# One scale per weight matrix, tiles split into their predecessor's slot, weight loads on SP, and a mixture product that goes through PSUM

## The chip, the core and the metric

The kernel runs on one core of a Trainium2 chip. The core has a matrix engine (PE, with its weight loads shown apart as PEld), three engines for elementwise work (DVE, ACT, POOL) and a queue for transfers (SP). ACT can issue transfers too. Each engine runs its own list of instructions in order, and semaphores make one wait for another. The metric is the device time of one execution in microseconds; lower is better. The kernel before takes 1015.41 us (median of 3 runs, 1015.3 to 1017.15).

## What is computed

Attention over 8 batches of 12 heads, 448 tokens and head size 64, and behind it a gated two-layer block with a token shift. Cut to what matters:

```python
def _attn_ref(q, k, v, g_q, g_k):
    q_n, k_n = (rmsnorm(q, g_q), rmsnorm(k, g_k))
    scores = scale * np.matmul(q_n, k_n.transpose(0, 1, 3, 2))
    attn = np.exp(scores - np.max(scores, axis=-1, keepdims=True))
    attn = attn / (np.sum(attn, axis=-1, keepdims=True) + 1e-09)
    return np.matmul(attn, v)

def _moe_ref(x, mu_k, mu_r, w_k, w_v, w_r):      # x: (8, 448, 768)
    x_prev = np.concatenate([np.zeros((B, 1, D)), x[:, :-1, :]], axis=1)
    xk = mu_k * x + (1.0 - mu_k) * x_prev
    xr = mu_r * x + (1.0 - mu_r) * x_prev
    k = np.maximum(xk @ w_k, 0.0)                # w_k: 768 x 1024
    v = k * k @ w_v                              # w_v: 1024 x 768
    r = 1.0 / (1.0 + np.exp(-(xr @ w_r)))        # w_r: 768 x 768
    return r * v
```

The three weight matrices arrive as float64, seen by the kernel as pairs of 32-bit integers. Products are made from two float16 parts of each operand (high and low), so every product of the block is three matmuls: high by high, high by low, low by high.

## The kernel before

The work is written as generators, one for each strand: loads of q and k, their norms (`stats`, `preps`), `scores`, `expo` and `probs`, `vpreps`, `attends`, the mixtures (`mixk`, `mixr`, `mix`), the weights (`wload`, `weights`, `wsplit`) and the block itself (`moe`). A planner (`Plan`) holds a clock for every engine and a price for every instruction. At each step it takes, of all strands, the instruction with the earliest key (engine free and operands ready, less a tenth of the strand's priority) and records it. So the order on each engine is fixed when the program is built, and any change of prices, strands or priorities moves instructions everywhere.

PE has to do, batch by batch: scores and products with v (attention), then for the block the products **K** (`xk` by w_k, 144 matmuls a batch), **R** (`xr` by w_r, 126) and **V** (`kk` by w_v, 168). `moe` (L1078) starts K of the first batch when its six mixtures and all eight tiles of w_k are there, and R of the first batch only when all 20 tiles of the three matrices are split (L1113, `wdone == NW`).

The weights come in 20 tiles of 128 columns: 8 of w_k, 6 of w_r, 6 of w_v. `wload` has ACT issue two transfers for each tile into buffers `raw` (two of its own; for w_k two more inside the tile `kk`, which is not needed yet). `weights` decodes each half: POOL takes the low bits out of a byte, ACT makes a float32 of the top word into a PSUM bank of the share `mm`, DVE joins both into a buffer `wf`. `wsplit` then finds one scale for each tile: PE forms the tile's product with itself, DVE takes its diagonal (`dg`), PE sums it by a matmul with ones, DVE takes the maximum and makes a power of two (`WSC`). Last, ACT and DVE (or, for the tiles in `POOL_TILES`, POOL, ACT and POOL) scale the tile and split it into its high and low parts, `wkh` and `wkl` and so on, which the block reads with a stride.

A mixture (`mix`, L951) is four instructions for each of 96 pieces of 128x448: POOL multiplies the shifted x by a column into `df`, DVE adds the other product onto it (both operands in SBUF), ACT makes the high part, POOL the low part.

The PSUM has eight banks. `Share` lets the strands hold some of them: five for scores (`sc`), two for the block and the decode (`mm`), two for products with v, norms of v and weights of w_k (`ot`).

Of the kernel before, what the change touches and what calls it, by code (L numbers as in the profile page):

```python
# [1 line left out]

# [29 lines left out]
WF_BUFS = 2  # L32
# [6 lines left out]
LOW_TILES = range(0, 20)  # L39
POOL_TILES = range(1, 14)  # L40
# [48 lines left out]
WB_A = 'ot'  # L89
WB_B = 'mm'  # L90
# [5 lines left out]
W_GAP = 10e3  # L96
# [108 lines left out]

class Plan:
    LAT = 35

    def __init__(self, tc):
        self.tc = tc  # L210
        self.clk = dict.fromkeys(("PE", "DVE", "ACT", "POOL", "SP"), 0.0)
        self.last, self.use, self.threads = {}, {}, []
        self.form, self.dma_free, self.acc, self.n = None, {"SP": 0.0, "ACT": 0.0}, False, 0
        self.held = {"DVE": [], "POOL": []}

# [13 lines left out]
    def spawn(self, gen, prio=0):  # L229
        th = [gen, prio, None, 0.0]  # L230
        self.threads.append(th)
        self.advance(th)
# [92 lines left out]
    def run(self):  # L325
        while self.threads:
            best, key = None, None
            for th in list(self.threads):
# [11 lines left out]
                k = max(self.clk[th[2][0].eng] + wait, th[3] + slack) - PS * (th[1]() if callable(th[1]) else th[1])  # L340
# [100 lines left out]
def attn_moe_kernel(tc, q, k, v, g_q, g_k, mu_k, mu_r, w_k, w_v, w_r, out):  # L441
# [15 lines left out]
    banks = {n: Share(psum, *c) for n, c in (("sc", SC_SHARE), ("mm", MM_SHARE), ("ot", OT_SHARE))}  # L457
# [18 lines left out]
    for nm, kt, n in (("wk", ND, D_FF), ("wr", ND, D_MODEL), ("wv", NF, D_MODEL)):  # L476
        WS[nm] = (wpool.tile([P, kt, n], F16, name=nm + "h"), wpool.tile([P, kt, n], F16, name=nm + "l"))
# [9 lines left out]

    def WB(ci):
        return WB_A if ci < NF else WB_B

# [9 lines left out]
    def late():  # L500
# [21 lines left out]
        "raw": Ring(stage, [P, NF // 2, 2 * P], I32, "raw", RAW_BUFS, plan),  # L522
# [4 lines left out]
    for name, plan_ in (("kk", KK_LENT), ("xk", XK_LENT)):  # L527
# [5 lines left out]
        for n in plan_:  # L533
# [10 lines left out]
            if len(r.shape) == 3:  # L544
# [27 lines left out]
    def mu_stats():  # L572
        yield from until(lambda: st["lu"] >= 1 and len(WFT))
# [377 lines left out]
    def mix(b, d, which, dst, df, cnt):  # L951
# [5 lines left out]
        yield G_.tensor_scalar(out=df, in0=xp, scalar1=sc[:, j + ND:j + ND + 1], scalar2=0.0, op0=ALU.mult, op1=ALU.add)  # L957
        yield V.scalar_tensor_tensor(out=df, in0=xc, scalar=sc[:, j:j + 1], in1=df, op0=ALU.mult, op1=ALU.add)
# [17 lines left out]
    def wload():  # L976
        for nm, w, kt, c, ci in WT:
            hk = kt // 2
            for i in range(0, kt, hk):
                yield from until(lambda: st["g"] >= W_G0 + W_G1 * ci and st["lu"] >= (LEAD_W if ci < W_L1 else LEAD_W + 1 if ci < W_L2 else LEAD_W + 2))  # L980
                raw = yield from R["raw"].get(ci < NF)
                yield A.dma_start(out=raw[:, 0:hk, :], in_=w[i * P:(i + hk) * P, c * P:(c + 1) * P].bitcast(I32).rearrange("(i p) n -> p i n", p=P))
                RAW[ci, i] = raw

    def weights():
        for nm, w, kt, c, ci in WT:
            f = yield from R["wf"].get(ci < NF)
            fi = f.bitcast(I32)
            hk = kt // 2
            for i in range(0, kt, hk):  # L990
                yield from until(lambda: (ci, i) in RAW and st["tq"] >= GATE_W)
                raw = RAW.pop((ci, i))
                r4 = raw[:, 0:hk, :].rearrange("p i (n two) -> p i n two", two=2)
                top, low = r4[:, :, :, 1], r4[:, :, :, 0]
                zb = yield from banks["mm"].get()
                z = zb[:, 0:hk * P].rearrange("p (i n) -> p i n", n=P)
                zi = z.bitcast(I32)
                if ci in LOW_TILES:
                    yield G_.tensor_scalar(out=low, in0=raw.bitcast(mybir.dt.uint8)[:, 0:hk, :].rearrange("p i (n b) -> p i n b", b=8)[:, :, :, 3], scalar1=-15.5, scalar2=2.0 ** -5, op0=ALU.add, op1=ALU.mult)
                    yield A.activation(out=z, in_=top.bitcast(F32), func=AF.Prelu, scale=F64_EXP, alpha=F64_NEG)  # L1000
                    yield V.scalar_tensor_tensor(out=fi[:, i:i + hk, :], in0=zi, scalar=3, in1=low, op0=ALU.logical_shift_left, op1=ALU.bitwise_or)
                else:
                    yield A.activation(out=z, in_=top.bitcast(F32), func=AF.Prelu, scale=F64_EXP, alpha=F64_NEG)
                    yield V.tensor_scalar(out=zi, in0=zi, scalar1=3, scalar2=None, op0=ALU.logical_shift_left)
                    yield V.scalar_tensor_tensor(out=fi[:, i:i + hk, :], in0=low, scalar=29, in1=zi, op0=ALU.logical_shift_right, op1=ALU.bitwise_or)
                R["raw"].put(raw)
                banks["mm"].put(zb)
            WFT[ci] = f
            plan.spawn(wsplit(nm, kt, c, ci, f), wprio)
# [4 lines left out]
    def wsplit(nm, kt, c, ci, f):  # L1014
        cs = slice(c * P, (c + 1) * P)
        wh, wl = WS[nm]
        f = f[:, 0:kt, :]
        w16 = f.bitcast(BF16).rearrange("p i (n two) -> p i n two", two=2)[:, :, :, 1]
        pg = yield from banks[WB(ci)].get()
        yield [T.matmul(form=("w", 110 * kt), out=pg[:, 0:P], lhsT=w16[:, i, :], rhs=w16[:, i, :], start=(i == 0), stop=(i == kt - 1)) for i in range(kt)]  # L1020
        sc = WSC[:, ci:ci + 1]
        sci = sc.bitcast(I32)
        dg = small.tile([P, P], F32, name="dg", bufs=1)
        yield V.tensor_tensor(out=dg, in0=pg[:, 0:P], in1=ident, op=ALU.mult)
        yield T.matmul(form=("f", 400), out=pg[:, P:2 * P], lhsT=ones.broadcast_to([P, P]), rhs=dg, start=True, stop=True)
        yield V.tensor_reduce(out=sc, in_=pg[:, P:2 * P], axis=AX.X, op=ALU.max)
        banks[WB(ci)].put(pg)
        yield V.tensor_scalar(out=sci, in0=sci, scalar1=24, scalar2=23, op0=ALU.logical_shift_right, op1=ALU.logical_shift_left)
        yield V.tensor_scalar(out=sci, in0=sci, scalar1=-1.0, scalar2=float(204 << 23), op0=ALU.mult, op1=ALU.add)
        if ci in POOL_TILES:  # L1030
            yield G_.tensor_scalar(out=f, in0=f, scalar1=sc, scalar2=0.0, op0=ALU.mult, op1=ALU.add)
            yield A.copy(out=wh[:, :, cs], in_=f)
            yield G_.tensor_tensor(out=wl[:, :, cs], in0=f, in1=wh[:, :, cs], op=ALU.subtract)
        else:
            yield A.activation(out=wh[:, :, cs], in_=f, func=AF.Copy, scale=sc)
            yield V.scalar_tensor_tensor(out=wl[:, :, cs], in0=f, scalar=sc, in1=wh[:, :, cs], op0=ALU.mult, op1=ALU.subtract)
        R["wf"].put(WFT.pop(ci))
# [40 lines left out]
    def moe():  # L1078
        wk, wr, wv = WS["wk"], WS["wr"], WS["wv"]
        kk = xr = None  # L1080
        for b in range(B):
# [23 lines left out]
            for f in range(NF):  # L1105
                fs = slice(f * P, (f + 1) * P)
                z = yield from banks["mm"].get()
                yield from prod(z[:, 0:S], lambda i, a: wk[a][:, i, fs], lambda i, c: xk[:, i, c, :], ND, S)
# [10 lines left out]
            for blk in range(1 - b % 2, NT, 2):  # L1119
# [5 lines left out]
                for h in range(2):  # L1125
                    hs = slice(h * NH, (h + 1) * NH)
                    zr = yield from banks["mm"].get()
                    yield from prod(zr[:, 0:NH], lambda i, a: xr[:, i, a, ts], lambda i, c: wr[c][:, i, hs], ND, NH)
# [4 lines left out]
                    yield from prod(zv[:, 0:NH], lambda i, a: kk[:, i, a, ts], lambda i, c: wv[c][:, i, hs], NF, NH)  # L1133
# [41 lines left out]
def layouts(inputs):  # L1175
# [29 lines left out]
    return {"q": qd, "k": kd, "v": vd.reshape(b * h // 2, P, 2 * n * HD)}  # L1205
# [32 lines left out]
```

## Time and profile before

| what | value |
|---|---|
| median of 3 runs | 1015.41 us |
| profiled execution, its own time | 1015.21 us |
| span of its instructions | 1013.4 us |
| DVE, ACT, POOL busy | 812.7, 746.0, 691.8 us |
| matmuls recorded | 6082 |

The page of the profile gives, for each engine, the busy time in the span, and then the span cut into 40 slices of 25.3 us with one digit each (9 is 90 per cent or more busy). Other views group instructions by kind, list them in order of time, or give every engine's busy time in a stretch. The times of single instructions overlap at their ends on one engine, so a sum of durations is larger than the busy time: over this run DVE's durations sum to 962 us and it was busy for 812.7.

### The profile page before, as it was taken

The numbers are of one execution on the slowest core, as the hardware profiler recorded it, in microseconds if no ns is written. First come the engines' busy times: TensorE is split into PE (matmuls) and PEld (weight loads), VectorE is DVE, ScalarE is ACT, GpSimd is POOL, SyncE is SP. The second block draws the span as 40 slices with busy tenths as digits, with TensorE's granted clock in tenths as the row PEclk, the third lists the DMA queues.
The fourth block names the chain that finished last, engine by engine and source line by source line (L and its number), as shares of the span: only waits on it lengthen the run. The fifth ranks groups of instructions, "written<-read, shape, count | busy, mean of one in ns | idle before, by whom it ended". The sixth has DMA issues, their size and how long they took to land. (4 is left out here: it accounts for less than half of the span.)

```text
span 1013.4 us, 18593 instructions
## 1 busy us (share of the span) xinstructions
PE 926.0 (91%) x6082; PEld 485.8 (48%) x6082; DVE 812.7 (80%) x2260; ACT 746.0 (74%) x1756; POOL 691.8 (68%) x734
## 2 busy tenths in 40 slices
PE   2588869669999999999999999899999999999998
PEld 2354434335544555455545555355545454455564
DVE  5879998999998698979997998799997989763000
ACT  3667878878788789888887887878886988952311
POOL 2787889743798747877886859855987478556501
PEclk9878979869999999999999999999999999999999
DMA  7322349667788789569847977869858884640000
GB/s 248 119 80 86 118 120 221 170 166 169 172 165 168 143 197 203 133 152 201 207 105 173 214 158 161 161 131 201 175 126 177 186 183 110 146 107 32 1 32 32
DMA packets 371138, 148.17 MB, mean 146 GB/s; under 512 B 338272, under 2 KB 355168, under 8 KB 371040
## 3 DMA queue, kind: packets, MB, share of 16 engines
q1 hardware_dynamic: 351792, 129.20, 57.0%
q10 hardware_dynamic: 19248, 17.77, 5.9%
q8 instruction: 48, 0.79, 0.3%
q14 instruction: 50, 0.41, 0.1%
HBM read 51.98 MB, written 11.01 MB: 62 GB/s over the span
## 5 line engine op out<-in xcount | busy, mean ns | idle before, releaser
L273 PE MATMUL ps<-wvh,kk 128*128 128x384 f16 x896 | 233.1, 326 | 0.8 <-DVE nat L273 0.8
L273 ACT ACTIVATE ps<-ps,sums 128x448 f32<-128x448 f32 x294 | 181.9, 621 | 52.5 <-DVE sums L273 48.9
L273 PE MATMUL ps<-xk,wkh 128*128 128x448 f16 x768 | 210.5, 356 | 4.8 <-DVE wf L273 3.9
L273 DVE SCALAR_TENSOR_TENSOR nat<-ps,sums,nat 128x64 f16<-128x64 f32 x480 | 190.7, 439 | 19.2 <-ACT nat L273 17.8
L273 DVE TENSOR_REDUCE sums<-ps 128x1 f32<-128x448 f32 x336 | 193.7, 612 | 15.4 <-PE ps L273 15.1
L273 PE MATMUL ps<-wrh,xr 128*128 128x384 f16 x672 | 179.9, 331 | 2.1 <-DVE nat L273 2.0
L273 ACT ACTIVATE nat<-ps,sums 128x448 f16<-128x448 f32 (+1 forms) x272 | 167.8, 659 | 16.9 <-DVE sums L273 7.1
L273 PEld LDWEIGHTS <-kk 128*128 128x128 f16 (+1 forms) x1362 | 129.2, 98 | 98.7 <-issue 13.5
L273 PE MATMUL ps<-stk 64*128 64x448 f16 (+3 forms) x1104 | 134.2, 390 | 26.4 <-ACT xk L273 6.2
L273 PE MATMUL ps<-wvl,kk 128*128 128x384 f16 x448 | 146.0, 326 | 0.0
L273 PE MATMUL ps<-xk,wkl 128*128 128x448 f16 x384 | 136.5, 355 | 0.0
L273 PEld LDWEIGHTS <-xr 128*128 128x128 f16 x1008 | 96.4, 99 | 80.1 <-issue 16.9
L273 PE MATMUL ps<-wrl,xr 128*128 128x384 f16 x336 | 111.1, 331 | 0.0
L273 PEld LDWEIGHTS <-wkh 128*128 128x128 f16 x768 | 71.9, 99 | 81.6 <-issue 21.6
L273 POOL TENSOR_TENSOR o<-o,bsc 128x384 f32<-128x384 f32 x48 | 43.3, 902 | 88.3 <-DVE o L273 52.3
L273 DVE SCALAR_TENSOR_TENSOR o<-o,ps 128x384 f32<-128x384 f32 x56 | 30.5, 545 | 87.7 <-PE ps L273 59.2
L273 PE MATMUL ps<-pT,vh 128*64 128x448 f16 x588 | 93.8, 363 | 1.4 <-DMA pT<-nat 0.7
L273 ACT ACTIVATE o<-ps,bsc 128x128 f32<-128x128 f32 x144 | 45.6, 387 | 51.2 <-PE ps L273 33.1
L273 POOL TENSOR_TENSOR qk<-qk,ss 128x896 f32<-128x896 f32 x36 | 64.0, 1778 | 22.1 <-DVE ss L273 14.9
L273 PEld LDWEIGHTS <-stk 64*128 64x128 f16 x1008 | 35.0, 98 | 78.0 <-issue 35.5
L273 DVE SCALAR_TENSOR_TENSOR df<-x,bsc,df 128x448 f32<-128x448 f32 x68 | 61.0, 910 | 5.8 <-POOL df L273 5.7
L273 POOL TENSOR_TENSOR nat<-nat 128x448 f32<-128x448 f32 x41 | 48.2, 1175 | 23.6 <-ACT nat L273 17.1
(161 smaller groups left out, 1813.7 us busy)
## 6 DMA issues: line engine op xcount, KB each, us to landing
vf<-in_v_dram SPq DMA_DIRECT2D x48, 256.0 KB, 3.0
out_dram<-o SPq DMA_DIRECT2D x28, 384.0 KB, 2.7
qk<-in_k_dram SPq DMA_DIRECT2D x23, 448.0 KB, 4.4
qk<-in_q_dram SPq DMA_DIRECT2D x22, 448.0 KB, 4.3
raw<-in_moe_w_v_dram ACTq DMA_DIRECT2D x12, 512.0 KB, 4.2
raw<-in_moe_w_r_dram ACTq DMA_DIRECT2D x12, 384.0 KB, 3.3
kk<-in_moe_w_k_dram ACTq DMA_DIRECT2D x8, 384.0 KB, 3.9
raw<-in_moe_w_k_dram ACTq DMA_DIRECT2D x8, 384.0 KB, 3.7
```

What stands on the lines that cost most here:

```text
L273: r = op.fn(op.kw["out"], op.kw["value"]) if op.fn.__name__ == "memset" else op.fn(**op.kw)
```

## The change

1. **Scales.** The products of all tiles of a matrix with themselves are summed in one PSUM bank (w_k: four blocks of columns of one bank), and `wscale` makes one scale for the matrix when its last tile has been decoded. The three instructions on a diagonal and the matmul with ones run 3 times and not 20.
2. **Slots.** A decoded tile waits for its scale, so all tiles of a matrix must be held. Tile c is decoded, as float32, into the slot of the split tile c + 1, which has just its size; the last tile goes to a `wf` buffer (now one, not two). `wsplit` takes the tiles in order, so tile c is split into slot c when tile c - 1 has been read from there. The slots of a matrix are now one tile `wk` (`wr`, `wv`), laid out by tile, part, row block and column.
3. **Loads.** The host lays the weights out by tile, so that each half tile is one run in every partition, and SP issues these 40 transfers, not ACT.
4. **Decode.** POOL writes the low bits straight to the place of the result, not back into `raw`, and `raw` is free once POOL, ACT and DVE are through. The PSUM banks of the decode are a share of their own (`wz`, two), as are the sums (`pg`, one).
5. **Split.** The tiles that POOL splits are now every second one (10), before tiles 1 to 13 (13).
6. **Mixture.** The first product is made by ACT into a PSUM bank (share `df`, one); DVE reads it from there.
7. **Planner.** Up to 20 ns of seeded noise is added to each key, and `W_GAP` goes from 10e3 to 7e3, so that the weights' priority falls by less with each tile.

```diff
-WF_BUFS = 2
+WF_BUFS = 1
-LOW_TILES = range(0, 20)
-POOL_TILES = range(1, 14)
+WZ_SHARE = (2, 0)
+PG_SHARE = (1, 0)
+DF_SHARE = (1, 0)
+POOL_TILES = range(0, 20, 2)
-WB_A = 'ot'
-WB_B = 'mm'
-W_GAP = 10e3
+W_GAP = 7e3
...
+SEEDS = [641]
+AMP = 20.0
+SEG = 1e9
...
+        th[4] = self.noise()
...
-                k = max(self.clk[th[2][0].eng] + wait, th[3] + slack) - PS * (th[1]() if callable(th[1]) else th[1])
+                k = max(self.clk[th[2][0].eng] + wait, th[3] + slack) - PS * (th[1]() if callable(th[1]) else th[1]) + th[4]
...
-        WS[nm] = (wpool.tile([P, kt, n], F16, name=nm + "h"), wpool.tile([P, kt, n], F16, name=nm + "l"))
+        WS[nm] = wpool.tile([P, n // P, 2, kt, P], F16, name=nm)
...
-        yield G_.tensor_scalar(out=df, in0=xp, scalar1=sc[:, j + ND:j + ND + 1], scalar2=0.0, op0=ALU.mult, op1=ALU.add)
-        yield V.scalar_tensor_tensor(out=df, in0=xc, scalar=sc[:, j:j + 1], in1=df, op0=ALU.mult, op1=ALU.add)
+        pb = yield from banks["df"].get()
+        yield A.activation(out=pb[:, 0:S], in_=xp, func=AF.Copy, scale=sc[:, j + ND:j + ND + 1])
+        yield V.scalar_tensor_tensor(out=df, in0=xc, scalar=sc[:, j:j + 1], in1=pb[:, 0:S], op0=ALU.mult, op1=ALU.add)
+        banks["df"].put(pb)
...
-                yield A.dma_start(out=raw[:, 0:hk, :], in_=w[i * P:(i + hk) * P, c * P:(c + 1) * P].bitcast(I32).rearrange("(i p) n -> p i n", p=P))
+                yield SP.dma_start(out=raw[:, 0:2 * hk * P], in_=w[c, h].bitcast(I32))
...
+                f = WS[nm][:, c + 1].rearrange("p a i n -> p (a i n)").bitcast(F32)
...
+            yield [T.matmul(form=("w", 110 * kt), out=pg[:, c % nb * P:(c % nb + 1) * P], lhsT=w16[:, i, :], rhs=w16[:, i, :], start=(c == 0 and i == 0), stop=(last and i == kt - 1)) for i in range(kt)]
+            if last:
+                plan.spawn(wscale(nm, kt, ci - c, ci + 1, pg, nb * P), wprio)
...
+    def wscale(nm, kt, c0, c1, pg, w):
+        sc = WSC[:, c0:c0 + 1]
...
+        yield V.tensor_copy(out=WSC[:, c0 + 1:c1], in_=sc.broadcast_to([P, c1 - c0 - 1]))
+        for ci in range(c0, c1):
+            plan.spawn(wsplit(nm, kt, ci - c0, ci, ci + 1 == c1), wprio)
+
+    def wsplit(nm, kt, c, ci, last):
+        yield from until(lambda: st["wdone"] == ci)
+        sc = WSC[:, ci:ci + 1]
+        f = WFT[nm].rearrange("p i n -> p (i n)")[:, 0:kt * P] if last else WS[nm][:, c + 1].rearrange("p a i n -> p (a i n)").bitcast(F32)
+        hi, lo = (WS[nm][:, c, a].rearrange("p i n -> p (i n)") for a in range(2))
```

What this does to the order is seen best at three places. The first is PE's list around the first product K of the first batch. Before, it stands here, behind scores (`stk`) and the sum of one tile's diagonal (`dg`):

```order
L273 LDWEIGHTS stk_948
L273 MATMUL ps_1447<-stk_948 64x448
L273 MATMUL ps_1421<-dg,ones 128x128
L273 LDWEIGHTS wkh
L273 MATMUL ps_1509<-xk_104,wkh 128x448
```

Now it stands behind the product of the very last weight tile with itself (`wf_1500`, the sixth of w_v), three transposes and the third and last sum of a diagonal:

```order
L287 LDWEIGHTS wf_1500
L287 MATMUL ps_1190<-wf_1500 128x128
L287 MATMUL ps_1588<-ident,nat_1436 128x128 x3
L287 MATMUL ps_1190<-dg,ones 128x128
L287 LDWEIGHTS wk
L287 MATMUL ps_1627<-xk_101,wk 128x448
```

So all 20 tiles are decoded ahead of the first K, where before 12 were, and no more products or sums for weights stand between K and R. On PE's list, ahead of the first K stand 78 score matmuls before and now, and 48 products with v; ahead of the first R stand 162 score matmuls and 114 products with v before, and 114 and 70 now.

The second place is DVE's list at the end of the weights, which the first R waits for. Before, the last tile of w_v has its own diagonal, maximum and two steps of its scale in between attention's work:

```order
L273 TENSOR_TENSOR dg<-ps_2413,ident 128x128
L273 TENSOR_SCALAR bstat<-bstat 128x1
L273 SCALAR_TENSOR_TENSOR nat_2401<-ps_2355,sums_109,nat_2401 128x64
L273 SCALAR_TENSOR_TENSOR nat_2401<-ps_2355,sums_109,nat_2401 128x384
L273 TENSOR_REDUCE WSC<-ps_2413 128x1
L273 TENSOR_SCALAR sums_110<-ps_2404 128x2
L273 TENSOR_REDUCE sums_105<-ps_2436 128x1
L273 TENSOR_SCALAR WSC<-WSC 128x1
```

Now the last splits of w_v stand between the mixtures for R (`df` from `x` and a PSUM bank), with no scale left to make:

```order
L287 SCALAR_TENSOR_TENSOR wv<-wf_1500,WSC,wv 128x1024
L287 TENSOR_SCALAR WIN<-WSC 128x12
L287 TENSOR_SCALAR sums_106<-ps_1876 128x2
L287 SCALAR_TENSOR_TENSOR df_1919<-x_1227,bsc,ps_1920 128x448
L287 TENSOR_SCALAR WIN<-WIN,smu 128x6
L287 TENSOR_SCALAR WIN<-WIN,wsc 128x6
```

The row `WIN<-WSC` was number 535 of DVE's list and is now number 377. Up to and with the output scales of the first batch, the last DVE work ahead of the first R, DVE now has 400 instructions.

The third place is SP's list near the start. These rows are new between the loads of q, k and v: each weight load waits until its buffer has been decoded, and the loads below wait with it.

```order
L287 DMA qk_134<-in_q_dram 128x896
L287 DMA kk_100<-in_moe_w_k_dram 128x768 x2
L287 DMA raw_255<-in_moe_w_k_dram 128x768
L287 DMA raw_264<-in_moe_w_k_dram 128x768
L287 DMA qk_205<-in_k_dram 128x896
L287 DMA kk_100<-in_moe_w_k_dram 128x768
L287 DMA xk_101<-in_q_dram 128x896
```

Before, the weight loads stood in ACT's list, between its arithmetic, and SP's list held q, k and v one behind the other:

```order
L273 DMA vf_95<-in_v_dram 128x512
L273 DMA qk_119<-in_k_dram 128x896
L273 DMA qk_159<-in_q_dram 128x896
L273 DMA qk_180<-in_k_dram 128x896
L273 DMA xk_104<-in_q_dram 128x896
L273 DMA qk_315<-in_k_dram 128x896
```

What moved is the order in which SP comes to the q and k of the second and third group of heads: one to four weight transfers now stand ahead of each.

More of the change, by code (lines that the diff above doesn't have):

```diff
@@ L985, in weights @@
     def weights():
         for nm, w, kt, c, ci in WT:
-            f = yield from R["wf"].get(ci < NF)
-            fi = f.bitcast(I32)
[L989 to L1005, printed above, removed]
@@ new lines, in weights @@
+            if c == 0:
+                pg = yield from banks["pg"].get()
+            last = ci + 1 in (NF, NF + ND, NW)
+            nb = 4 if ci < NF else 1
+            if last:
+                wf = yield from R["wf"].get(ci < NF)
+                f = wf.rearrange("p i n -> p (i n)")[:, 0:kt * P]
+                WFT[nm] = wf
+            else:
+                f = WS[nm][:, c + 1].rearrange("p a i n -> p (a i n)").bitcast(F32)
+            fi = f.bitcast(I32)
+            for h in range(2):
+                yield from until(lambda: (ci, h) in RAW and st["tq"] >= GATE_W)
+                raw = RAW.pop((ci, h))
+                n = kt * P // 2
+                cols = slice(h * n, (h + 1) * n)
+                zb = yield from banks["wz"].get()
+                z = zb[:, 0:n]
+                yield G_.tensor_scalar(out=fi[:, cols], in0=raw.bitcast(mybir.dt.uint8)[:, 0:8 * n].rearrange("p (n b) -> p n b", b=8)[:, :, 3], scalar1=-15.5, scalar2=2.0 ** -5, op0=ALU.add, op1=ALU.mult)
+                yield A.activation(out=z, in_=raw[:, 0:2 * n].rearrange("p (n two) -> p n two", two=2)[:, :, 1].bitcast(F32), func=AF.Prelu, scale=F64_EXP, alpha=F64_NEG)
+                yield V.scalar_tensor_tensor(out=fi[:, cols], in0=z.bitcast(I32), scalar=3, in1=fi[:, cols], op0=ALU.logical_shift_left, op1=ALU.bitwise_or)
+                banks["wz"].put(zb)
@@ L1011, in inverse @@
     def inverse(o, i):
         return V.tensor_scalar(out=o.bitcast(I32), in0=i.bitcast(I32), scalar1=-1.0, scalar2=float(0x7F000000), op0=ALU.mult, op1=ALU.add)
[L1014 to L1021, printed above, removed]
-        sci = sc.bitcast(I32)
[L1023 to L1027, printed above, removed]
+    def wscale(nm, kt, c0, c1, pg, w):
+        sc = WSC[:, c0:c0 + 1]
+        sci = sc.bitcast(I32)
+        dg = small.tile([P, 4 * P], F32, name="dg", bufs=1)[:, 0:w]
+        yield V.tensor_tensor(out=dg.rearrange("p (b n) -> p b n", n=P), in0=pg[:, 0:w].rearrange("p (b n) -> p b n", n=P), in1=bcast(ident[:, :], w // P), op=ALU.mult)
+        yield T.matmul(form=("f", 200 + 1.7 * w), out=pg[:, 0:w], lhsT=ones.broadcast_to([P, P]), rhs=dg, start=True, stop=True)
+        yield V.tensor_reduce(out=sc, in_=pg[:, 0:w], axis=AX.X, op=ALU.max)
+        banks["pg"].put(pg)
@@ L1037, in wsplit @@
-        R["wf"].put(WFT.pop(ci))
+            yield A.copy(out=hi, in_=f)
+            yield G_.tensor_tensor(out=lo, in0=f, in1=hi, op=ALU.subtract)
+        else:
+            yield A.activation(out=hi, in_=f, func=AF.Copy, scale=sc)
+            yield V.scalar_tensor_tensor(out=lo, in0=f, scalar=sc, in1=hi, op0=ALU.mult, op1=ALU.subtract)
+        if last:
+            R["wf"].put(WFT.pop(nm))
         st["wdone"] += 1
```

52 lines of the change are left out of this document (29 added, 23 removed).

## The prediction

> **What bounds the kernel now.** I read the page first, for the engine that is nearly full and the part of the span in which it isn't.
>
> ```profile
> span 1013.4 us, 18593 instructions
> PE 926.0 (91%) x6082; PEld 485.8 (48%) x6082; DVE 812.7 (80%) x2260; ACT 746.0 (74%) x1756; POOL 691.8 (68%) x734
> PE   2588869669999999999999999899999999999998
> PEclk9878979869999999999999999999999999999999
> ```
>
> PE is busy for 91% of the span, and its digits fall below 9 almost only in the first ten slices, 250 us. There its granted clock is also below full. So I looked for what PE does there, in its list in order of time, at three places (start, length, and in brackets the idle time before it with what ended it):
>
> ```profile
> 141.01 0.91 PE L273 MATMUL ps<-xk,wkh 128*128 128x448 f16 x2 [3.90 <-DVE wf L273]
> 227.46 0.50 PE L273 MATMUL ps<-wrh,xr 128*128 128x384 f16 x1 [1.39 <-DVE nat L273]
> 1008.30 0.33 PE L273 MATMUL ps<-wvh,kk 128*128 128x384 f16 x1
> ```
>
> These are the first K, the first R and the last V. They cut the run into stages, and the view of busy time by stretch gives each engine's part in them (start:end, length, then busy us and instructions of each engine, granted clock, DMA share, GB/s).
>
> ```profile
> core 0: us, PE busy (x) PEld busy (x) DVE busy (x) ACT busy (x) POOL busy (x), PEclk, DMA share, GB/s
> 0.00:141.00 141.00, 93.55 (x531) 53.77 (x532) 117.70 (x337) 92.63 (x215) 99.38 (x132) 0.88 0.40 128
> 141.00:186.80 45.80, 41.90 (x253) 21.64 (x253) 39.11 (x101) 38.49 (x82) 43.12 (x42) 0.94 0.76 179
> 186.80:227.50 40.70, 24.56 (x152) 11.84 (x150) 37.55 (x109) 31.02 (x65) 22.57 (x25) 0.68 0.73 181
> 227.50:926.00 698.50, 683.34 (x4666) 351.32 (x4667) 609.90 (x1704) 565.70 (x1355) 496.28 (x506) 0.99 0.74 161
> 926.00:1008.60 82.60, 82.60 (x485) 47.24 (x483) 7.84 (x11) 18.14 (x43) 29.67 (x32) 1.00 0.05 20
> 1008.60:1013.40 4.80, 0.03 (x1) 0.00 (x0) 0.56 (x1) 0.00 (x0) 0.83 (x1) 1.00 0.20 82
> ```
>
> From the first R on, PE is the bound: 683.34 of 698.50 us, then all of 82.60, and a tail of 4.80 us. Ahead of it PE waits. The stretch from 186.8 us, where the last K of batch 0 has begun, to the first R is the worst: 40.70 us with 24.56 busy, at a clock of 0.68, while DVE is busy for 37.55. What PE waits for there is the weights, which DVE finishes in between attention. So the end is **the time of the first R, plus PE's work after it, plus the tail**. I work out each.
>
> **Term 1, the first K.** The order gives the first K the sixth mixture as its last operand, which is DVE instruction 335 now and was 338. The durations of what differs:
>
> ```profile
> L273 DVE SCALAR_TENSOR_TENSOR wf<-ps,raw 128x384 int32<-128x384 int32 x18 | 9.8, 547 | 0.1
> L273 DVE SCALAR_TENSOR_TENSOR wf<-ps,raw 128x512 int32<-128x512 int32 x12 | 8.2, 680 | 0.6 <-issue 0.4 <-POOL raw L273 0.2
> L273 DVE SCALAR_TENSOR_TENSOR wkl<-kk,WSC,wkh 128x768 f16<-128x768 f32 x1 | 1.0, 1008 | 0.0
> L273 DVE TENSOR_TENSOR dg<-ps,ident 128x128 f32<-128x128 f32 x20 | 5.6, 280 | 0.8 <-PE ps L273 0.8
> L273 DVE TENSOR_REDUCE WSC<-ps 128x1 f32<-128x128 f32 x20 | 5.7, 283 | 2.6 <-PE ps L273 2.5
> L273 DVE TENSOR_SCALAR WSC<-WSC 128x1 int32<-128x1 int32 x40 | 5.8, 144 | 0.2
> L273 DVE SCALAR_TENSOR_TENSOR df<-x,bsc,df 128x448 f32<-128x448 f32 x68 | 61.0, 910 | 5.8 <-POOL df L273 5.7
> L273 DVE SCALAR_TENSOR_TENSOR dfx<-x,bsc,dfx 128x448 f32<-128x448 f32 x28 | 31.6, 1130 | 4.1 <-POOL dfx L273 4.1
> L273 DVE SCALAR_TENSOR_TENSOR df<-x,bsc,df x68: 653/700/2564, 127.3 to 930.1; 128x448 f32<-128x448 f32 x68
> ```
>
> DVE gains 12 decodes of w_v halves (12 x 0.680) and 4 more of w_k and w_r (4 x 0.547), 10.3 us, and 6 splits of about 1.0 us. It loses 8 to 10 diagonals and maxima and 16 steps of scales (10 x 0.280 + 8 x 0.283 + 16 x 0.144, less 0.6 for a wide one: 6.8). The mixture's DVE part has a mean of 974 ns (68 x 910 and 28 x 1130) but a least of 653 and a median of 700 (last row): POOL's work lengthens it, since both of its operands are in SBUF. With one in PSUM no row here shows it; I bound it by 653 and the mean, 974, and take 660, near the least, because instructions that read PSUM show no such spread (547 and 680 above). Six mixtures: less 1.9 us. A few norms and copies more, about 4. Together about +12 us of durations; DVE's durations overlap (962 for 812.7 busy), so +10 us, and **the first K at 151 us**.
>
> The Trainium skill, SBUF — State Buffer, Who interferes with whom, says that a DVE instruction with two SBUF inputs contends with a GpSimd instruction that reads SBUF, and one with a single SBUF input doesn't. The trace agrees as far as it goes (653 to 2564 ns for two inputs); by that rule the 660 holds, without it the first R comes 4 us later (12 mixtures).
>
> **Term 2, from the first K to the first R.** Before, 45.80 us to the last K, then 40.70. In the new order nothing of weights is left for PE, and the R follows the last K directly. PE's groups in 141 to 186.8:
>
> ```profile
> L273 PE MATMUL ps<-wf 128*128 128x128 bf16 x28 | 2.4, 220 | 0.5 <-DVE wf L273 0.5
> L273 PE MATMUL ps<-dg,ones 128*128 128x128 f32 x8 | 1.7, 300 | 2.1 <-DVE dg L273 2.1
> L273 PE MATMUL ps<-ident,nat 128*128 128x128 f32 x14 | 2.2, 277 | 0.0
> ```
>
> Of the 45.80 us, 2.4 and 1.7 for weights with 2.6 of waits are gone, and a third of the transposes (0.8): 38 us. In these 38 us DVE has to do 65 instructions, with five splits of weights and six mixtures for R, where it did 101 in 45.8; it keeps up. ACT, 84% busy there, gets the mixtures' six products (3.5 us) and sheds tile splits. So I let PE set the pace: **the first R at 189 us**. Bounds: 176 if DVE alone counts (147 fewer instructions than the 547 to 227.5, 44 us less of 194.4 busy, at the same share of the time), and 201 if ACT's work to that point (about 143 us against 162.1) takes the same share of the time as now.
>
> **Term 3, from the first R to the last V.** Now 1008.6 - 227.5 = 781.1 us. Attention that stood ahead of the first R now stands behind it: 48 score matmuls, 44 products with v, 16 transposes. Their pace, from two places in PE's list:
>
> ```profile
> 237.05 0.38 PE L273 MATMUL ps<-pT,vh 128*64 128x448 f16 x2
> 239.26 0.34 PE L273 MATMUL ps<-wvh,kk 128*128 128x384 f16 x1
> 257.93 1.31 PE L273 MATMUL ps<-stk 64*128 64x448 f16 x12
> 259.17 0.34 PE L273 MATMUL ps<-wrh,xr 128*128 128x384 f16 x1
> ```
>
> 22 products in 2.21 us and 12 scores in 1.24, 0.1 us each: 9.2 us, and 16 transposes at a third of their 277 ns or so, 1.8. Term 3 is **792 us** if PE stays the bound. Whether it does is for ACT: 84 mixtures are left, each with an ACT product that no row shows. The nearest:
>
> ```profile
> L273 ACT ACTIVATE ps<-raw 128x384 f32<-128x384 f32 x20 | 10.6, 528 | 0.3 <-issue 0.3
> L273 ACT ACTIVATE ps<-raw 128x512 f32<-128x512 f32 x12 | 7.7, 638 | 1.3 <-DVE wf L273 0.9 <-DVE WSC L273 0.3
> 510.00:520.00 10.00, 10.00 (x65) 4.62 (x63) 9.84 (x24) 10.00 (x25) 10.00 (x9) 1.00 0.29 75
> ACT ps L273 <- DVE sums L273: 44.3, 40, 5.4
> ```
>
> They bound it by 528 and 638 ns; 580 for 448 columns. That is 49 us, and attention put off adds about 20 (16 exponentials and 16 copies of 0.62 to 0.66): ACT goes from 565.7 to 635 us of 710, from 81% to 89%. It can run that full: in 510 to 520 us ACT and PE are both busy for all of it, and its greatest wait (last row, 227 to 926 us) is for DVE's maxima, 44.3 us, on a DVE that is relieved (84 x 0.31 = 26 us). POOL loses 84 products of 0.66 us and more. I take nothing off or on for this; the rivals carry both ends.
>
> **The rest.** The last V to the end: 4.8 us. The planner's noise takes no time on the chip; its effect is in the order, which is counted. The 40 issues of weight loads leave ACT's list for SP's. One from ACT's queue in the order of time:
>
> ```profile
> 19.81 0.37 ACTq L273 DMA_DIRECT2D kk<-in_moe_w_k_dram  x1
> ```
>
> At 0.37 us they make 15 us of ACT's time ahead of 227 us; I take nothing for it, since PE and DVE set the pace there. **Sum: 189 + 792 + 4.8 = 986 us of span.** The profiled execution took 1015.21 for a span of 1013.4, so 1.8 more: **988 us**, against 1015.21 (and the median of 1015.41, the same within 0.2).
>
> **Rivals.**
>
> *Loads wait on SP* (15%). Weight loads now wait on SP for ACT's, POOL's and DVE's decode, and behind them stand q, k and v and later transposes. Against: their data are needed late, and SP mostly sits idle. For:
>
> ```profile
> qk<-in_k_dram SPq DMA_DIRECT2D x23, 448.0 KB, 4.4
> raw<-in_moe_w_k_dram ACTq DMA_DIRECT2D x8, 384.0 KB, 3.7
> ```
>
> A load takes 4.4 us and a weight half 3.7, so a load kept behind four of them comes some 15 us late; if that hits the first 150 us once, 1003 us. The Trainium skill, DMA: Bandwidth & Descriptors, Queues, rings and completion order, says that SP and ACT each have a ring on every DMA engine, consumed in ring order; so weights would now also hold up the data of the loads behind them. No run here shows that yet; by it this rival's price is the same 15 us.
>
> *ACT becomes the bound* (9%, slower). If ACT can't be busier than the 81% it has now, its 635 us take 784 and not 710, and the end is 988 + 74 = 1062. It decides at 86%: 635/0.86 = 738, 28 later, which eats the whole gain. The 10 of 10 us above speak against it.
>
> *The weights don't come earlier* (6%, slower). No tile is split before its matrix is whole, so if the last split of w_v is late the first R stays at 227 us, with 11 us of attention put off: 227.5 + 792 + 6.6 = 1026. Against it: DVE has 400 instructions up to there, and had 547.
>
> *Relief* (15%). PE's 15.2 us of idle time in 227.5 to 926 shrink by half with a DVE and POOL that block each other less, and the first R comes at 182: 974.
>
> *No effect* (5%): a gain of the start is lost later in new waits for PSUM banks, of which the decode, sums and mixtures hold four: within 2 us of 1015.
>
> **Numbers.** The forecast, 980 to 996, has 50%. The range leaves out the 20% of ACT, the late weights and no effect: 971 to 1012. A measurement of this kernel can tell about 0.2% from no change. Faster by more: 50 + 15 + 15 = 80%; the same 5%; slower 15%.
>
> **What would show it.** First K near 151 and first R near 189 us in PE's list; a clock above 0.9 and PE idle for no more than 5 us between them; DVE's mixture near 660 ns, ACT's near 580; ACT near 89% and PE still near 98% from the first R to the last attention; some 92 more attention matmuls there. A first R behind 201 us, or an ACT that ends PE's waits, would make it wrong.

## The result, and the profile after

The changed kernel takes **1022.59 us** (median of 4 runs, 1021.35 to 1023.0), the kernel before 1015.76 us in runs beside it (4 runs, 1015.3 to 1017.15): a ratio of 1.0063, 95% interval 1.0045 to 1.008. So it is slower by more than the 0.2% that can be told from no change, where 988 us and a gain had been forecast. The lines of the page that answer to those of before (the span, the busy time of each engine, and PE and its clock in 40 slices, now of 25.5 us):

```profile
span 1021.0 us, 18527 instructions
PE 918.5 (90%) x6048; PEld 482.0 (47%) x6048; DVE 785.4 (77%) x2200; ACT 792.6 (78%) x1850; POOL 605.5 (59%) x632
PE   2767868899899999898999999999999999999998
PEclk9798969999899999999999999999999999999999
```

PE has less to do than before (918.5 against 926.0 us), and DVE and POOL much less. The hole of the start ends a slice earlier. But behind the tenth slice PE's row, which had one 8 there (and the last slice), now has three. The first K and the first R of the changed kernel in PE's list, and its stages (start:end, length, busy us and instructions of each engine, granted clock, DMA share, GB/s):

```profile
157.93 0.55 PE L287 MATMUL ps<-xk,wk 128*128 128x448 f16 x1 [2.34 <-DVE df L287]
199.58 0.50 PE L287 MATMUL ps<-wr,xr 128*128 128x384 f16 x1
...
0.00:157.90 157.90, 100.26 (x580) 55.95 (x580) 130.44 (x336) 106.24 (x240) 102.45 (x137) 0.88 0.51 166
157.90:199.60 41.70, 37.45 (x212) 18.02 (x213) 36.23 (x76) 37.38 (x76) 36.78 (x32) 0.95 0.28 69
199.60:901.20 701.60, 665.68 (x4576) 341.32 (x4575) 605.89 (x1767) 619.79 (x1466) 430.17 (x425) 0.99 0.76 166
901.20:1016.20 115.00, 115.00 (x684) 66.74 (x683) 12.25 (x22) 29.20 (x71) 35.28 (x40) 1.00 0.05 21
1016.20:1021.00 4.80, 0.06 (x1) 0.00 (x0) 0.55 (x1) 0.00 (x0) 0.83 (x1) 1.00 0.20 82
```

And the stage from the first R to the last attention in the kernel before, cut in the same way (last attention at 906.8 us):

```profile
227.50:907.10 679.60, 664.44 (x4549) 339.93 (x4549) 603.98 (x1695) 560.24 (x1340) 488.72 (x495) 0.99 0.76 165
```

The first R comes at 199.6 us, 27.9 earlier. From there to the end of the last V the kernel before needs 781.1 us and this one 816.6, 35.5 more. Two parts make that up. PE's busy time there goes from 765.9 us (the prediction's rows) to 665.68 + 115.00 = 780.7: 14.8 more. And its idle time between the first R and the last attention goes from 679.60 - 664.44 = 15.2 to 701.60 - 665.68 = 35.9: **20.7 us of new waits**. Who ends them (PE's waits in this stage: us in total, times, longest):

```profile
PE ps L287 <- DVE nat L287: 13.4, 21, 1.7
PE ps L287 <- ACT vh L287: 4.2, 3, 2.9
PE ps L287 <- DVE sums L287: 3.0, 2, 2.2
```

In the kernel before the list was led by these two, and PE waited for `nat` 6 times in the stage, not 21 (`natx`, the same work in one more buffer, 4 times then and 3 now):

```profile
PE ps L273 <- DMA stk<-natx: 5.7, 2, 3.8
PE ps L273 <- DVE nat L273: 4.3, 6, 1.4
```

So now there are many small waits, for the splits of the probabilities (`nat`) above all, and no great one. DVE is no busier than before there (605.89 in 701.60). So DVE is late, not overworked.

### The profile page after: what moved, and what is told of

The parts are those of the page before. It is cut to its first block, busy times and chain, and to the rows that moved or that the text cites. A ratio compares the mean times of both kernels' runs of the same rounds, so it can differ in the third digit from the quotient of the medians.

```text
span 1021.0 us, 18527 instructions
## 1 busy us (share of the span) xinstructions
PE 918.5 (90%) x6048; PEld 482.0 (47%) x6048; DVE 785.4 (77%) x2200; ACT 792.6 (78%) x1850; POOL 605.5 (59%) x632
## 5 line engine op out<-in xcount | busy, mean ns | idle before, releaser
L287 PE MATMUL ps<-wv,kk 128*128 128x384 f16 x1344 | 234.0, 326 | 1.4 <-DVE nat L287 1.4
L287 PE MATMUL ps<-xk,wk 128*128 128x448 f16 x1152 | 230.3, 356 | 5.3 <-DVE df L287 2.3
L287 DVE SCALAR_TENSOR_TENSOR nat<-ps,sums,nat 128x64 f16<-128x64 f32 (+1 forms) x500 | 198.7, 441 | 25.4 <-ACT nat L287 24.3
L287 ACT ACTIVATE nat<-ps,sums 128x448 f16<-128x448 f32 (+1 forms) x280 | 172.2, 663 | 19.0 <-DVE sums L287 12.3
L287 PE MATMUL ps<-wr,xr 128*128 128x384 f16 x1008 | 177.6, 328 | 1.5 <-ACT nat L287 0.6
L287 PEld LDWEIGHTS <-wk 128*128 128x128 f16 (+1 forms) x1194 | 113.3, 99 | 124.5 <-issue 20.4
L287 PEld LDWEIGHTS <-xr 128*128 128x128 f16 x1008 | 96.5, 98 | 74.2 <-issue 12.6
L287 PEld LDWEIGHTS <-stk 64*128 64x128 f16 x1008 | 35.9, 98 | 86.5 <-issue 43.7
L287 ACT ACTIVATE ps<-x,bsc 128x448 f32<-128x448 f32 x96 | 63.5, 668 | 3.7 <-POOL x L287 1.9
L287 PE MATMUL ps<-pT,vl 128*64 128x448 f16 x336 | 61.6, 358 | 0.0
L287 POOL TENSOR_TENSOR kf<-kf 128x448 f32<-128x448 f32 x46 | 42.9, 934 | 30.6 <-ACT kk L287 30.5
L287 POOL TENSOR_TENSOR nat<-qk,nat 128x896 f16<-128x896 f32 x25 | 47.2, 1888 | 16.9 <-ACT nat L287 16.9
```

Of the source, the lines that this page charges most:

```text
L287: r = op.fn(op.kw["out"], op.kw["value"]) if op.fn.__name__ == "memset" else op.fn(**op.kw)
```

## Experiments

The stage from the first R to the last attention is called the main stage from here on, and PE's idle time in it is its length less PE's busy time, from the row of that stage in each trace. Theory A said that ACT, which got the products, holds PE; theory B that the planned order does; theory C that DVE is the tight partner.

### The product's engine, the order, and the noise

**The product on POOL, the order kept.** The planner prices and orders the product as ACT's, and then records it for POOL. All other instructions stay in their places.

```diff
-        yield A.activation(out=pb[:, 0:S], in_=xp, func=AF.Copy, scale=sc[:, j + ND:j + ND + 1])
-        yield V.scalar_tensor_tensor(out=df, in0=xc, scalar=sc[:, j:j + 1], in1=pb[:, 0:S], op0=ALU.mult, op1=ALU.add)
+        yield swap(A.activation(out=pb[:, 0:S], ...), G_.tensor_scalar(out=df, in0=xp, ...))
+        yield swap(V.scalar_tensor_tensor(..., in1=pb[:, 0:S], ...), V.scalar_tensor_tensor(..., in1=df, ...))
```

> The changed kernel with every engine's order kept, but the mixture's first product made by POOL into df in SBUF, as before, and not by ACT into PSUM. Theory A, ACT is what holds PE in the main stage (first R to last attention): ACT's busy time there falls from 619.8 us by about 50, PE's idle time from 35.9 to about 15 us as before, and the time from 1022.6 to about 1002 us. Theory B, the planned order holds PE, whoever makes the product: idle stays above 30 us, 1017 to 1027 us. Theory C, DVE is the tight partner: its mixture goes back from 673 to about 970 ns, PE's idle time grows, over 1027 us.

Measured: 1057.06 us (ratio 1.0411, 1.0396 to 1.0427), PE idle for 58.5 us in the main stage though ACT is 37 us less busy there. Theory A falls; it came out as C had it, though the run doesn't separate DVE's longer mixtures from POOL's fuller list (493.0 us busy in place of 430.2). DVE's mixture, in the changed kernel and here (groups by kind: count, busy, mean ns of one):

```profile
L287 DVE SCALAR_TENSOR_TENSOR df<-x,bsc,ps 128x448 f32<-128x448 f32 x69 | 46.2, 673 | 9.2 <-ACT ps L287 6.6 <-POOL xk L287 1.9
```

```profile
L294 DVE SCALAR_TENSOR_TENSOR df<-x,bsc,df 128x448 f32<-128x448 f32 x69 | 82.3, 1197 | 12.6 <-POOL df L294 12.3
```

**The same, planned anew** (the product is POOL's for the planner too, and no PSUM bank is taken).

```diff
-        pb = yield from banks["df"].get()
-        yield A.activation(out=pb[:, 0:S], ...)
-        yield V.scalar_tensor_tensor(..., in1=pb[:, 0:S], ...)
-        banks["df"].put(pb)
+        yield G_.tensor_scalar(out=df, in0=xp, ...)
+        yield V.scalar_tensor_tensor(..., in1=df, ...)
```

> The changed kernel with part 6 undone and the order planned anew (POOL makes the product, no PSUM bank for it). Theory A: about 1000 us, idle of PE in the main stage near 15 us. Theory B: as far from 1022.6 as another order brings it, and not the time of the run with the order kept; 1005 to 1035 us. First R near 200 us by both.

Measured: 1033.33 us (1.0175, 1.016 to 1.019), idle 44.2 us. The same work in another order is 24 us faster: B has a large part.

**The kernel before with the product on ACT, the order kept** (into `df` in SBUF, since no bank is free).

```diff
-        yield G_.tensor_scalar(out=df, in0=xp, ...)
+        yield swap(G_.tensor_scalar(out=df, in0=xp, ...), A.activation(out=df, in_=xp, func=AF.Copy, ...))
```

> The kernel before with every engine's order kept, but the mixture's first product made by ACT into df in SBUF, and not by POOL. Theory A: ACT gains 77 x 0.56 = 43 us in the main stage, PE's idle time there goes from 15 to about 35 us, 1035 us. Theory B: within 4 us of 1015.8. Theory C: DVE's mixture gets shorter without POOL beside it (974 to below 850 ns), PE idle below 12 us, 1005 to 1012 us.

Measured: 1025.84 us (1.0103, 1.0085 to 1.0121), idle 21.7 us: about half the loss that A asked for, with a third of the idle time. An order suits the engine for which it was planned: here POOL's product was the better, in the changed kernel's order ACT's.

**No noise.**

```diff
-SEEDS = [641]
+SEEDS = [0]
```

> The changed kernel, planned without noise, nothing else. Theory A: the same work for ACT, within 5 us of 1022.6, idle of PE in the main stage 30 to 40 us. Theory B: the order decides, over 5 us from 1022.6 on either side, with PE's idle time moved by as much.

Measured: **1001.92 us** (0.987, 0.9854 to 0.9887), 20.7 us faster than the change and 13 faster than before. The noise costs more than the whole loss; without it the change is a gain. Its page and its stages:

```profile
span 999.6 us, 18563 instructions
PE   1787867999899999999999999999999999999998
...
0.00:155.40 155.40, 97.35 (x555) 51.79 (x556) 125.20 (x327) 107.04 (x243) 98.87 (x134) 0.87 0.49 158
155.40:198.40 43.00, 41.91 (x271) 20.86 (x271) 35.60 (x86) 40.89 (x83) 38.22 (x33) 0.97 0.61 128
198.40:880.70 682.30, 659.60 (x4548) 338.60 (x4547) 599.19 (x1765) 613.41 (x1456) 431.07 (x428) 0.99 0.79 169
880.70:994.80 114.10, 114.10 (x678) 66.18 (x678) 12.25 (x22) 29.16 (x71) 33.36 (x38) 1.00 0.06 22
```

The first R is at 198.4 us, as with the noise. Idle in the main stage is 22.7 us and not 35.9, and PE's work from the first R on 773.7 us and not 780.7, about half of that because 34 matmuls of attention more stand ahead of the first R (12 scores and 22 products with v, 0.1 us each); the other half isn't traced. ACT is *fuller* (613.41 of 682.30, 90%), so its load was not what held PE. ACT and DVE wait less for each other. Their groups in the main stage, of the change and then without noise (exponentials; sums and splits of the probabilities; at the end the idle time ahead of them and what ended it):

```profile
L287 ACT ACTIVATE ps<-ps,sums 128x448 f32<-128x448 f32 x278 | 172.1, 621 | 64.5 <-DVE sums L287 54.4 <-DVE stm L287 5.8 <-DVE ss L287 1.3
L287 DVE TENSOR_SCALAR sums<-ps 128x2 f32<-128x2 f32 x139 | 21.3, 153 | 30.8 <-ACT ps L287 30.4
L287 DVE SCALAR_TENSOR_TENSOR nat<-ps,sums,nat 128x64 f16<-128x64 f32 x235 | 64.2, 276 | 24.6 <-ACT nat L287 23.6
```

```profile
L287 ACT ACTIVATE ps<-ps,sums 128x448 f32<-128x448 f32 x274 | 172.4, 633 | 40.5 <-DVE sums L287 37.9 <-DVE stm L287 0.6 <-ACT ps L287 0.2
L287 DVE TENSOR_SCALAR sums<-ps 128x2 f32<-128x2 f32 x138 | 21.0, 152 | 22.7 <-ACT ps L287 22.5
L287 DVE SCALAR_TENSOR_TENSOR nat<-ps,sums,nat 128x64 f16<-128x64 f32 x217 | 59.8, 276 | 16.0 <-ACT nat L287 13.2 <-POOL natx L287 1.4 <-issue 0.5
```

One way in which 20 ns can do this is seen in the order. Scores come in groups of two halves, each with a maximum on DVE and an exponential on ACT; the next step needs both halves of the oldest group. Strands of one kind that wait for the same engine have *exactly the same key* in the planner, since the engine's clock is the greater term for all of them. Without noise the oldest goes first. With it, chance decides: of the 5578 steps of the plan 627 take another strand than the keys without noise would, 436 of them between equal keys. DVE's list of the change, where the `sums` of a group has one number:

```
L287 TENSOR_REDUCE sums_106<-ps_4789 128x1
L287 TENSOR_REDUCE sums_107<-ps_4818 128x1
L287 TENSOR_REDUCE sums_106<-ps_4788 128x1
L287 TENSOR_REDUCE sums_107<-ps_4817 128x1
```

Those four on the chip (order of time, DVE's maxima and ACT's exponentials):

```profile
403.39 1.15 DVE L287 TENSOR_REDUCE sums<-ps 128x1 f32<-128x448 f32 x2
404.48 0.67 ACT L287 ACTIVATE ps<-ps,sums 128x448 f32<-128x448 f32 x1
405.25 1.16 DVE L287 TENSOR_REDUCE sums<-ps 128x1 f32<-128x448 f32 x2 [0.71 <-ACT ps L287]
406.44 0.61 ACT L287 ACTIVATE ps<-ps,sums 128x448 f32<-128x448 f32 x1 [0.67 <-DVE sums L287]
408.94 0.61 ACT L287 ACTIVATE ps<-ps,sums 128x448 f32<-128x448 f32 x1
410.89 0.64 ACT L287 ACTIVATE ps<-ps,sums 128x448 f32<-128x448 f32 x1
```

The older group has its first maximum at 403.39 and its last exponential at 410.89 to 411.53, behind both of the younger: 8.1 us, the longest of all in the main stage. Over the 138 groups of the main stage (from the instructions of DVE and ACT, matched in order to the planner's strands) the time from the first maximum to the last exponential has a mean of 3.02 us, and 2.55 without noise (about 2.4 in the kernel before). In the whole list of maxima on DVE a half of a younger group stands directly ahead of one of an older group 23 times, in that of exponentials on ACT 25 times; without noise never.

### Is it this seed, or any noise?

**Weight loads on ACT, the order kept.** It goes with the rival of loads that wait on SP.

```diff
-                yield SP.dma_start(out=raw[:, 0:2 * hk * P], in_=w[c, h].bitcast(I32))
+                yield swap(SP.dma_start(out=raw[:, 0:2 * hk * P], ...), A.dma_start(out=raw[:, 0:2 * hk * P], ...))
```

> The changed kernel with the order of all arithmetic and all other transfers kept, but the 40 weight loads issued by ACT at their place in the order, not by SP. If loads on SP delay the start, the first R comes earlier than 199.6 us by 5 or more and the time falls below 1018 us. If SP's queue costs nothing, the first R stays within 3 us of 199.6 or is late by what the 40 issues cost ACT (up to 15 us), 1020 to 1037 us.

Measured: 1021.14 us (1.0054, 1.0039 to 1.0069), first R at 197.2. The first R comes 2.4 us earlier, with the issues that ACT now pays for counted in: SP's queue costs the start little, not 15 us. The 1.5 us of the whole time are not clear of noise (the interval of the change is 1.0045 to 1.008).

**Another seed** (`SEEDS = [1]`).

> The changed kernel, planned with another seed of the noise. By the planner's own clock this order ends 21.5 us later than that of the change (971.1 against 949.6). Theory B1, any noise costs about 20 us against no noise: 1015 to 1030 us. B2, orders scatter and the change's seed was an unlucky draw: anything from 995 to 1015 us. B3, the chip follows the planner's clock: about 1044 us (1022.6 + 21.5).

Measured: 1041.99 us (1.0261, 1.0245 to 1.0276), first R at 197.7, idle 48.7 us. Among the two seeds the planner's clock was right, as B3 had it: 19.4 us later, 21.5 by the plan. But it is no guide from noise to none: without noise the plan ends 2.1 us *later* than the change's (951.7 against 949.6), and the chip was 20.7 earlier. So of the two seeds that were run, the change's is the better one; B2 is not borne out.

**POOL's product without noise** (the edit of the replanned run above, with `SEEDS = [0]`).

> The changed kernel with part 6 undone (POOL makes the product), planned without noise. It stands to the run without noise (1001.9 us) as the replanned one (1033.3) to the change (1022.6). If the product on ACT is a gain by itself, 10 to 30 us slower than 1001.9: 1012 to 1032 us; its DVE mixture has a mean near 950 ns in place of 673. If ACT is what holds PE, faster than 1001.9.

Measured: 1007.68 us (0.9931, 0.9904 to 0.9958), idle 23.4. Noise costs this variant 25.6 us (1033.33 against it). And the mixture's part is worth 5.8 us without noise, as far as two orders can be compared.

**The kernel before with the noise** (`noise` and the term in the key, as in the change).

> The kernel before, planned with the change's noise (the same seed and size), nothing else. By the planner's clock it ends 5.7 us later (983.6 against 977.9). B1: 1030 to 1040 us. B2: 1003 to 1028 us, with the difference in PE's idle time. B3: about 1021 us.

Measured: 1052.61 us (1.0368, 1.0345 to 1.039), idle 37.9 us, first R at 236.0: 37 us slower, beyond all that was expected. The noise alone, with no other edit, is a loss. The main stage, to be held against the 679.60 us with 664.44 busy of the kernel before:

```profile
236.00:959.70 723.70, 685.83 (x4675) 352.46 (x4675) 617.44 (x1718) 572.44 (x1364) 494.04 (x500) 0.99 0.73 157
```

### Ties, or near keys? Whose list?

**Ties alone** (`AMP = 1e-6` for 20).

> The changed kernel with the same seed, but noise of a millionth of a nanosecond in place of 20 ns, so that it decides only between strands with exactly the same key (451 of 5578 steps then take another strand than the oldest). Theory T, the loss is that halves of younger groups go ahead of halves of older ones: 1015 to 1035 us as with the full noise, first maximum to last exponential of a group near 2.9 us in place of 2.5. Theory N, the loss comes from the 191 steps in which a strand with a later key goes ahead: within 8 us of 1001.9, groups near 2.5 us.

Measured: 1047.51 us (1.0318, 1.0284 to 1.0351), idle 46.7, groups at 2.88 us. Reordering equal keys is enough for the loss, and costs more than theory T had asked for.

**Ties kept.**

```diff
-                k = max(...) - PS * (...) + th[4]
+                k = max(...) - PS * (...)
+                k += tie.setdefault(k, th[4])
```

> The changed kernel with its noise of 20 ns, but strands with exactly the same key share the noise of the oldest, so that the oldest still goes first. Theory T: 995 to 1012 us, groups near 2.5 us. Theory N: 1015 to 1035 us.

Measured: 1029.99 us (1.0148, 1.0117 to 1.0179), idle 35.7, though groups take 2.64 us and never stand out of order (186 steps of this plan take another strand, none between equal keys). So theory T, as the only one, falls: near keys cost as well, and broken groups are one way of it, not the whole. PE's waits look different too: for `nat` 8.1 us in 6 waits, the longest 4.6, where the change had 13.4 us in 21, the longest 1.7.

**Dearer prices in the planner, no noise.**

```diff
+        c = c + 16 if ps else 1.08 * c + 60
         return c, c + 80
...
-            return c + 52, c + 170
+            return c + 70, c + 188
```

> The changed kernel, planned without noise and with dearer prices for DVE's and ACT's work in the planner (DVE from SBUF alone 8 per cent and 60 ns more, from PSUM 16 ns more, ACT with a running sum 18 ns more), about half of what the trace shows above the prices. If PE's remaining idle time of 22.7 us in the main stage comes from prices that are too low: below 998 us, idle near 15 us. If the order is as good as it gets by prices: within 6 us of 1001.9.

Measured: 1002.28 us (0.9879, 0.9849 to 0.991): idle falls to 15.0 us as expected, but the first R comes at 215.5. It gains 7.7 of waits and loses 17.1 at the start, and PE's work behind is 8.5 us less: no gain.

**The gap of before, no noise** (`W_GAP = 10e3`).

> The changed kernel, planned without noise and with the weights' gap of 10e3 as before, so that the weights lose priority faster. If the gap is what brings the weights early: first R later than 198.4 us by 8 or more, with more attention ahead of it, and the time within 6 us of 1001.9 or above it. If it does nothing: first R within 3 us, time within 5 us of 1001.9.

Measured: 1032.16 us (1.0169, 1.0127 to 1.0212), first R at 236.0, idle 28.8. The smaller gap is what brings the weights early; without it the rest of the change is a loss.

**Noise on PE's keys alone, and on all others alone.**

```diff
-        th[4] = self.noise()
+        th[4] = self.noise() if isinstance(x, list) and x[0].eng == "PE" else 0.0
```

> The changed kernel, with the noise added to the keys of PE's work alone. If the loss comes from PE's list: PE's idle time from the first R to the last attention over 33 us and 1018 us or more. If it comes from the other engines' lists: idle near 23 us as without noise, 995 to 1010 us, and a group's first maximum to last exponential near 2.5 us.

> The changed kernel, with the noise added to the keys of all work but PE's. If the loss comes from the lists of DVE and ACT, where a younger group's half now stands directly ahead of an older one's 22 and 21 times: idle over 33 us, groups near 2.9 us, 1015 us or more. If it comes from PE's list: idle near 23 us, 995 to 1010 us.

Measured: 1022.48 us (1.0066, 1.0044 to 1.0089), idle 41.3, groups 2.58 us, and 1024.53 us (1.0085, 1.0061 to 1.0108), idle 35.5, groups 2.88. Either is enough. They do not tell one engine's list from the others. In the plan with noise on PE's keys only 60 of the 5578 steps take another strand than the keys without noise would, 3 of them between equal keys, and it still loses 20.6 us against no noise: few steps suffice.

**Part 6 alone on the kernel before, planned anew** (with a share `df` of one bank).

> The kernel before with part 6 alone (ACT makes the product into a PSUM bank of the share df), planned anew, no noise. From the pair without noise (POOL 1007.7, ACT 1001.9) a gain of about 6 us: 1009 us, with DVE's mixture near 670 ns. If ACT's load tells as in the run of the kernel before with the order kept (1025.8, product into SBUF): 1020 us or more.

Measured: 1026.34 us (1.0095, 1.0071 to 1.0119), idle 23.4, though DVE's mixture has its 673 ns. Part 6 loses there, as the second expectation had it, and gains in the changed kernel without noise: its sign hangs on the order.

**The change without noise, loads on ACT, the order kept.**

> The changed kernel, planned without noise, the order kept, but the 40 weight loads issued by ACT. From the pair with the change's order (1021.1 against 1022.6, first R 2.4 us earlier) 1 to 3 us faster than 1001.9: 999 to 1001 us. If that pair was chance: within 1 us of 1001.9, or slower by ACT's issues.

Measured: **997.97 us** (0.9818, 0.9796 to 0.984), first R at 195.2, the fastest of all and 4.0 us faster than with the loads on SP, a little more than expected. Its interval lies clear of that of the run without noise and with loads on SP (0.9854 to 0.9887).

All together, times in us; idle is PE's in the main stage:

| kernel | noise | first R | idle | time |
|---|---|---|---|---|
| before | no | 227.5 | 15.2 | 1015.76 |
| before, product on ACT, order kept | no | 227.0 | 21.7 | 1025.84 |
| before, part 6 planned | no | 226.7 | 23.4 | 1026.34 |
| change without noise, loads on ACT | no | 195.2 | 22.4 | 997.97 |
| change without noise | no | 198.4 | 22.7 | 1001.92 |
| the same, dearer prices | no | 215.5 | 15.0 | 1002.28 |
| the same, product on POOL | no | 199.8 | 23.4 | 1007.68 |
| the same, gap of before | no | 236.0 | 28.8 | 1032.16 |
| change, loads on ACT | 641 | 197.2 | 36.8 | 1021.14 |
| change, noise on PE | 641 | 191.3 | 41.3 | 1022.48 |
| **the change** | 641 | 199.6 | 35.9 | 1022.59 |
| change, noise on the rest | 641 | 201.0 | 35.5 | 1024.53 |
| change, ties kept | 641 | 209.9 | 35.7 | 1029.99 |
| change, product on POOL, planned | 641 | 200.1 | 44.2 | 1033.33 |
| change, seed 1 | 1 | 197.7 | 48.7 | 1041.99 |
| change, ties alone | 641 | 209.2 | 46.7 | 1047.51 |
| before with noise | 641 | 236.0 | 37.9 | 1052.61 |
| change, product on POOL, order kept | 641 | 204.9 | 58.5 | 1057.06 |

The eight kernels without noise have 15 to 29 us of idle time, the ten with it 35 us and more. Four of the eight without noise are planned in yet other orders (part 6 on the kernel before, dearer prices, the product on POOL, the gap of before), so another order alone doesn't bring the idle time above 35 us. The whole time is another matter: the gap of before costs 30 us without any noise, with a first R that comes 37.6 us later.

## Why the prediction was wrong

**The step that failed** is the sentence on the noise: that it "takes no time on the chip; its effect is in the order, which is counted". What was counted were the numbers of instructions ahead of the first K and the first R. The order *within* the main stage, where the sum left PE's idle time at the 15.2 us of the kernel before ("I take nothing off or on for this"), was not worked out, and there most of the noise's cost sits. The sign that the prediction named for it, PE near 98% busy from the first R to the last attention, is where it shows: 94.9% (665.68 of 701.60), and 96.7 without noise. The noise costs 21.4 us of span (1021.0 against 999.6): 13.2 of idle time, 7.0 of PE's work from the first R on, 1.2 at the first R. No rival named it. The nearest, no effect through a gain "lost later in new waits", had 5%, the wrong place (PSUM banks), and too small a loss.

**The first K, forecast 151, came at 157.9.** The terms were right: DVE's durations up to it grew by 12.6 us (forecast 12), decodes by 10.0 (10.3) and splits by 6.6 (6), scales less 4.7 (6.8). But they overlapped less than assumed (busy 12.7 more in the stage rows, not 10), and DVE's idle time, taken as unchanged, grew by 4.2 (27.5 against 23.3).

**The first R, forecast 189 with a bound of 201, came at 199.6.** From the first K 41.7 us, not 38: PE idles for 4.2 there, where the sum left 1.3 (3.9 in the same stage before, less 2.6). And R doesn't follow the last K directly: that ends at 195.2, and 2.5 us of the idle time are a wait for `nat` by scores between the two. It lies inside the bounds, close to the 201 that went by ACT's share; that ACT set it is not shown. Without noise it is 198.4, so the miss is not the noise's.

**Term 3, forecast 792, measured 816.6, and 796.4 without noise.** Its two halves: PE's work grew by 14.8 us where 11 were forecast for attention put off; the 48 scores, 44 products and 16 transposes are there (the transposes' 1.8 us would have been 1.5 by the prediction's own figures). The idle time was to stay and grew by 20.7, of which 7.5 are left without noise.

**The mixture.** DVE's part was forecast at 660 ns and measured at 673, from 651 to 683 in the main stage, where it had reached 2564 before. The rule of the Trainium skill (SBUF — State Buffer, Who interferes with whom), that a DVE instruction with one SBUF input doesn't contend with GpSimd, is borne out: the 70 of 96 mixtures that ran beside an instruction of POOL took 673 ns, the other 26 took 674. Before, with two SBUF inputs, it was 1075 ns for 72 beside POOL and 672 for the other 24. ACT's part was forecast at 580 ns and took 668. But 77 mixtures, not 84, stand in the main stage (as many as before), so that they made 51.0 us busy where 49 were forecast.

**ACT.** Forecast 89% busy in the main stage, measured 88.3 (619.79 of 701.60). The rival that it becomes the bound, deciding at 86%, is refuted by the run without noise, which is the faster one with ACT at 90%.

**Loads on SP**, a rival of 15 us: real but small, with 2.4 to 3.2 us at the first R and, in the one pair whose intervals part, 4 of the time. Whether data were held up behind weights, or only their issue on SP, these runs can't tell apart.

**Relief** did not come: PE's idle time in the main stage shrank in no run (15.0 with dearer prices, against 15.2 before).

**The sum.** 189 + 792 + 4.8 against 199.6 + 816.6 + 4.8: 10.6 of the 35.2 us are the start, 24.6 term 3. Without noise 13.8 would have been left (999.6 against 985.8); its 1001.92 lies inside the range of 971 to 1012, on the side that was forecast.

What stays open: why noise costs 13 us of idle time with ties kept, and 19 on PE's keys alone, when groups keep their order. The smaller gap was not run alone on the kernel before, so how much of the earlier first R is the gap's and how much that of parts 1 to 6 is not shown. Nor is it shown whether noise costs as much with other priorities in the planner: it was run with two seeds, on one planner. And whether the seed was chosen by the planner's own clock: that ends at 949.6 us for the change, 951.7 without noise and 960.6 to 971.1 for the seeds 1 to 8, so 641 is the best of these by it, but on the chip the order without noise is better. The chip's time is later than the planned end by 51 to 79 us in eight noisy orders (the change by 73), and by 38 to 56 in five without noise. That an order picked by its planned end has spent its slack is argued, not shown.

## What to carry to other kernels

Where a planner fixes the order of engines that run in order, its tie-break is part of the design: here equal keys are common, and chance in place of the oldest strand cost 45.6 us (1047.51 against 1001.92). Keeping the ties was not enough, since near keys cost as well (1029.99). A change that bundles a gain with a new order has to be measured once with the order's own change taken out; here the bundle lost 7 us while it gains 13 without the noise. An engine swap measured in a kept order says as much of the order as of the engines (34 us one way in one order, 10 the other way in another).

## What was not expected of the hardware

ACT's product with its source in SBUF costs about the same wherever it lands: 668 ns into PSUM (the change), and 684 into SBUF, in the kernel before with the order kept:

```profile
L280 ACT ACTIVATE df<-x,bsc 128x448 f32<-128x448 f32 x68 | 45.3, 684 | 1.1 <-POOL xr L280 0.7 <-DVE bsc L280 0.3
L280 DVE SCALAR_TENSOR_TENSOR df<-x,bsc,df 128x448 f32<-128x448 f32 x68 | 57.9, 858 | 13.7 <-ACT df L280 13.6
```

And DVE's mixture keeps a mean of 858 ns there although POOL has lost the products: the rest of POOL's work is enough to stretch it. Of all 96 mixtures of that run, both operands in SBUF, the 53 beside an instruction of POOL took 1027 ns and the other 43 took 677. With one operand in PSUM it is 673 either way.
